# The second layer's weight conversion: its low part subtracted by VectorE in place of GpSimd

## The chip, the cores and the metric

The kernel runs on one core of a Trainium2 chip. Its time is that of the device in microseconds (us). The engines are named as in the profile: PE is TensorE (PEld its weight loads), DVE is VectorE, ACT is ScalarE, POOL is GpSimd, SP is SyncE, whose queue issues the DMAs.

## The reference

A linear attention with a decay per channel, then two layers of a gated MLP over 3072 tokens, all in float32:

```python
batch, n_heads, seq, head_dim = (4, 8, 768, 48)
n_tokens, d_model, d_ff = (3072, 384, 2048)
for t in range(S):
    state = alpha[:, :, t, :, None] * state + np.einsum('bhd,bhe->bhde', k[:, :, t], v[:, :, t])
    y[:, :, t] = np.einsum('bhd,bhde->bhe', q[:, :, t], state)
# first layer, x: (3072, 384), w_in: (384, 2048), w_out: (2048, 384)
h = x @ w_in
g = h * (1.0 / (1.0 + np.exp(-1.702 * h)))
x = g @ w_out
# second layer, with weights of its own
h = x @ w_in
g = h - np.tanh(h)
out = g @ w_out
```

## The kernel before

**Steps.** Each layer takes its 3072 tokens in 6 blocks of 512, and `d_ff` in 16 parts of 128. One block and one part are a step; `s` counts them, 96 for the first layer (s = 0 to 95) and 96 for the second (96 to 191). A step multiplies the block by 128 columns of `w_in` (`gemm1`, L343), puts the result through the layer's nonlinearity and multiplies that by 128 rows of `w_out` (`gemm2`, L350), three steps later (`LAG = 3`). Three accumulators (banks) take the sums of `gemm2` over the 16 parts.

**Two parts of every number.** For precision each operand is kept as a high and a low part, and a product is three matmuls: high by high, low by high, high by low. So a step is 9 matmuls of `gemm1` and 9 of `gemm2`, all 128 x 128 by 128 x 512. The high part is a rounding copy by ACT, the low part the difference. For the weights these are `whi[m]` and `wlo[m]`, 16 tiles of 128 x 768 each (the part's columns of `w_in` and its rows of `w_out` side by side). There is one set of them: the second layer's part m takes the tile of the first layer's part m, once the last block's `gemm2` with it is done.

**Conversion of a weight tile.** The weights arrive as 64-bit floats (`raw`, three buffers), and `conv` makes float32 of them with three passes of DVE (`w_bits`, L160 and L161, and `w_join`, L173) into one of four buffers `cf` (the fourth is in `arena`). Then `w_split` takes them apart: ACT copies the high part (L190), and the low part is a subtraction (L191), which the change touches. The first layer's 16 tiles are converted while attention runs, the second's 16 tiles in the last block of the first layer and the first steps of the second, about one in a step.

**What else DVE does in a step.** In a first-layer step it finishes the activation (`sig_1`: ACT's tanh, L357, then DVE's L358, which reads the bank of `gemm1`). The bank is one of two, so `gemm1` of step s + 2 waits for L358 of step s. Then `g_split` makes `ghi` (ACT, L361) and `glo` (L362; on DVE in the last block), which `gemm2` of step s needs. In a second-layer step L369 and L370 on ACT and L371 to L373 on DVE take the place of L357 and L358. GpSimd makes the low part of the second layer's input (`xlo`, L410).

**Order.** Instructions are written in the order of the steps, and a scheduler in the compiler that simulates time sets each engine's queue from it. Within a queue the order is fixed: an instruction that waits holds all behind it.

Of the kernel before, what the change touches and what calls it, by code (L numbers as in the profile page):

```python
# [7 lines left out]
F32 = mybir.dt.float32  # L8
# [5 lines left out]
ALU = mybir.AluOpType  # L14
# [54 lines left out]
def linear_attention_mlps(ctx, tc, xq, xv, fa, fv, cst, w1, w2, out):  # L69
    nc = tc.nc  # L70
    V, A, G, P, SP = nc.vector, nc.scalar, nc.gpsimd, nc.tensor, nc.sync
# [5 lines left out]
    def T(name, shape, dt=F32):  # L77
        return sb.tile(list(shape), dt, name=name)

    whi = [T(f"whi{m}", (128, WC), F32R) for m in range(MT)]  # L80
    wlo = [T(f"wlo{m}", (128, WC), F32R) for m in range(MT)]
# [106 lines left out]
    def w_split(l, m):  # L188
        f = cfs[l][m % len(cfs[l])]
        A.copy(whi[m], f)  # L190
        (V if l == 1 else G).tensor_tensor(out=wlo[m], in0=f, in1=whi[m].bitcast(F32), op=ALU.subtract)  # L191

# [221 lines left out]
    def conv(layer, split=True):  # L416
        if split and cv[2] < cv[1]:
            w_split(layer, cv[2] % MT)
            cv[2] += 1
        if cv[1] < cv[0]:  # L420
            m = cv[1] % MT
            w_join(layer, m)
            cv[1] += 1
            if m + 3 < MT:
                w_load(layer, m + 3)
        if cv[0] < min(layer * MT, cv[2] + len(cfs[layer])):
            w_bits(layer, cv[0] % MT)
            cv[0] += 1
# [51 lines left out]
    def place(s):  # L480
        l, j, m = steps[s]
        i = j if l == 1 else len(L1) + j
        t0, n = (L1 if l == 1 else L2)[j]
        alt = i >= len(L1) - 1 and (i - len(L1)) % 2
        return l, j, m, i, t0, n, [bank[b] for b in ((5, 6, 7) if alt else (0, 1, 2))]

    for s in range(NS + LAG):
        if s:
            if s <= NS:
                l, j, m, i, t0, n, acc = place(s - 1)  # L490
                prev = s - 1, n, V if l == 2 or j in (0, len(L1) - 1) else G
        if s < NS:
            l, j, m, i, t0, n, acc = place(s)
# [44 lines left out]
        if s >= LAG:  # L538
            l, j, m, i, t0, n, acc = place(s - LAG)
# [108 lines left out]
```

## Time and profile before

| | |
|---|---|
| median of 3 runs | 989.65 us (988.11 to 989.95) |
| profiled execution, its own time | 989.62 us |
| span of its instructions | 987.6 us |
| PE busy | 946.0 us (96%) |
| DVE, ACT, POOL busy | 616.1, 459.6, 229.7 us |
| mean granted clock of PE | 0.995 of full speed |

The span runs from the first to the last instruction; the execution is 2.0 us longer. Busy shares are means over the span. Matmuls overlap: one takes about 0.40 us in the records, but the next starts 0.23 us after it, so PE's pace is read from the distance of starts, and gaps from its waits.

### The profile page before, as it was taken

What the parts mean: (1) busy time and instruction counts of PE and PEld (TensorE: products, weight loads), DVE (VectorE), ACT (ScalarE), POOL (GpSimd) and SP (SyncE); (2) the same over time, 40 slices, a digit from 0 to 9 for tenths busy, and PEclk for the clock granted to TensorE, in tenths of its full rate; (3) what the DMA queues carried; (4) which work ended last, traced back from release to release, by engine and by line L of the source; (5) the groups of instructions that cost most, each with busy time, mean ns of one, the idle gap of its engine ahead of it and who ended that gap; (6) DMA issues with size and microseconds to landing.
All of it is one profiled execution on the core that took longest, in us unless ns stands there. A gap on an engine that the chain in (4) does not pass through costs nothing.

```text
span 987.6 us, 13249 instructions
## 1 busy us (share of the span) xinstructions
PE 946.0 (96%) x4870; PEld 739.4 (75%) x4870; DVE 616.1 (62%) x898; ACT 459.6 (47%) x969; POOL 229.7 (23%) x166
## 2 busy tenths in 40 slices
PE   6869999999999999999999889999999999999997
PEld 4656787777777777777787668888888888888885
DVE  7999743441443453643159987676777777766663
ACT  4445434333444534333343445554565656544542
POOL 1221302433544444343425450100100101000000
PEclk9999999999999999999999999999999999999999
DMA  9795212332455443752124330020132430000001
GB/s 285 239 313 158 72 53 58 99 89 84 131 183 182 152 139 105 268 164 73 49 78 150 124 128 1 6 91 0 59 133 90 140 100 25 33 1 1 33 0 37
DMA packets 58044, 101.85 MB, mean 103 GB/s; under 512 B 4992, under 2 KB 37376, under 8 KB 57968
## 3 DMA queue, kind: packets, MB, share of 16 engines
q1 hardware_dynamic: 57968, 100.90, 32.1%
q8 instruction: 40, 0.66, 0.3%
q14 instruction: 36, 0.29, 0.1%
HBM read 86.73 MB, written 14.16 MB: 102 GB/s over the span
## 4 chain that ended last, share of the span: by engine, by line
PE 82%; DVE 11%; DMA 3%; issue 3%; SPq 1%; ACT 0%; DVEq 0%; ACTq 0%
PE bank L350 38%; PE bank L343 38%; PE bank L273 3%; PE bank L305 2%; DMA arena<-xq 2%; DVE cf L160 2%; DVE cf L173 2%; DMA raw<-w 1%; DVE arena L237 1%; PE bank L302 1%; DVE cf L161 1%; DVE glo L362 1%; PE bank L312 1%; DVE gt L358 1%; DVE arena L173 1%
## 5 line engine op out<-in xcount | busy, mean ns | idle before, releaser
L343 PE MATMUL bank<-xhi,whi 128*128 128x512 f32 x576 | 231.5, 402 | 10.7 <-DVE gt L358 7.9
L361 ACT CAST ghi<-gt 128x512 fp32r<-128x512 f32 x192 | 119.0, 620 | 244.9 <-DVE gt L373 136.3
L343 PE MATMUL bank<-xlo,whi 128*128 128x512 f32 x576 | 230.6, 400 | 0.0
L350 PE MATMUL bank<-ghi,whi 128*128 128x512 f32 x576 | 229.4, 398 | 0.0
L343 PE MATMUL bank<-xhi,wlo 128*128 128x512 f32 x576 | 229.4, 398 | 0.0
L350 PE MATMUL bank<-ghi,wlo 128*128 128x512 f32 x576 | 228.4, 397 | 0.0
L350 PE MATMUL bank<-glo,whi 128*128 128x512 f32 x576 | 227.3, 397 | 0.0
L362 DVE TENSOR_TENSOR glo<-gt,ghi 128x512 fp32r<-128x512 f32 x128 | 97.3, 760 | 82.2 <-ACT ghi L361 77.0
L358 DVE SCALAR_TENSOR_TENSOR gt<-gt,bank 128x512 f32<-128x512 f32 x96 | 65.5, 682 | 127.3 <-ACT gt L357 123.8
L343 PEld LDWEIGHTS bank<-xhi,whi 128*128 128x128 f32 x576 | 109.3, 190 | 41.2 <-DVE gt L358 10.2
L343 PEld LDWEIGHTS bank<-xlo,whi 128*128 128x128 f32 x576 | 109.4, 190 | 27.0 <-issue 1.4
L343 PEld LDWEIGHTS bank<-xhi,wlo 128*128 128x128 f32 x576 | 109.3, 190 | 25.9 <-issue 0.6
L350 PEld LDWEIGHTS bank<-ghi,whi 128*128 128x128 f32 x576 | 108.3, 188 | 27.1 <-issue 1.2
L350 PEld LDWEIGHTS bank<-glo,whi 128*128 128x128 f32 x576 | 108.1, 188 | 25.9 <-DVE arena L243 0.2
L350 PEld LDWEIGHTS bank<-ghi,wlo 128*128 128x128 f32 x576 | 108.3, 188 | 25.5 <-issue 0.8
L362 POOL TENSOR_TENSOR glo<-gt,ghi 128x512 fp32r<-128x512 f32 x64 | 85.4, 1334 | 142.8 <-ACT ghi L361 119.0
L237 DVE TENSOR_TENSOR_SCAN arena<-arena,seg 112x516 f32<-112x516 f32 x46 | 62.3, 1354 | 37.2 <-DMA arena<-xq 36.3
L371 DVE SCALAR_TENSOR_TENSOR arena<-arena,bank 128x512 f32<-128x512 f32 x96 | 65.7, 684 | 29.0 <-ACT arena L369 27.8
L410 POOL TENSOR_TENSOR xlo<-arena,xhi 128x512 fp32r<-128x512 f32 x18 | 27.5, 1555 | 236.4 <-ACT xhi L409 187.5
L357 ACT ACTIVATE gt<-bank 128x512 f32<-128x512 f32 x96 | 57.0, 594 | 51.8 <-PE bank L343 51.1
L373 DVE SCALAR_TENSOR_TENSOR gt<-arena 128x512 f32<-128x512 f32 x96 | 69.7, 726 | 10.6 <-DVE arena L372 0.9
L369 ACT ACTIVATE arena<-bank 128x512 f32<-128x512 f32 x96 | 57.2, 596 | 34.0 <-PE bank L343 33.3
(86 smaller groups left out, 895.4 us busy)
## 6 DMA issues: line engine op xcount, KB each, us to landing
raw<-w SPq DMA_DIRECT2D x64, 768.0 KB, 4.6
arena<-xq SPq DMA_DIRECT2D x46, 224.0 KB, 3.0
arena<-xq SPq DMA_DIRECT2D x22, 451.5 KB, 5.6
xt<-arena SPq DMA_DIRECT2D x96, 48.0 KB, 2.9
xlo<-xt SPq DMA_DIRECT2D x24, 192.0 KB, 4.2
x1t<-xs SPq DMA_DIRECT2D x6, 768.0 KB, 5.2
arena<-x1t SPq DMA_DIRECT2D x6, 768.0 KB, 4.5
out<-xs SPq DMA_DIRECT2D x18, 256.0 KB, 2.3
```

Of the source, the lines that this page charges most:

```text
L173: V.scalar_tensor_tensor(out=f.bitcast(I32), in0=r[:, :, 0], scalar=29, in1=f.bitcast(I32), op0=ALU.logical_shift_right, op1=ALU.bitwise_or)
L237: V.tensor_tensor_scan(out=dec(g, n), data0=src(g, n), data1=seg, initial=0.0, op0=ALU.mult, op1=ALU.max)
L273: P.matmul(out=o[hh][:, i], lhsT=k[r, 2 * x + i], rhs=q[r, 2 * x + i], start=True, stop=True)
L343: P.matmul(out=h, lhsT=w[m][:, ws], rhs=x[:, k, :n], start=c == 0, stop=c == 3 * KT - 1)
L350: P.matmul(out=acc[k][:, :n], lhsT=w[m][:, ws], rhs=x[s % 3][:, :n], start=m == 0 and c == 0, stop=m == MT - 1 and c == 2)
L357: A.activation(out=th[i][:, :n], in_=h, func=AF.Tanh, scale=0.851)
L358: V.scalar_tensor_tensor(out=gf[i][:, :n], in0=th[i][:, :n], scalar=1.0, in1=h, op0=ALU.add, op1=ALU.mult)
L361: A.copy(ghi[s % 3][:, :n], gf[s % 2][:, :n])
L362: e.tensor_tensor(out=glo[s % 3][:, :n], in0=gf[s % 2][:, :n], in1=ghi[s % 3][:, :n].bitcast(F32), op=ALU.subtract)
L369: A.activation(out=u, in_=h, func=AF.Square, accum_out=usum[:, s - NS1 :][:, :1])
L371: V.scalar_tensor_tensor(out=p, in0=u, scalar=P3, in1=h, op0=ALU.mult, op1=ALU.mult)
L373: V.scalar_tensor_tensor(out=gf[i], in0=w, scalar=PD, in1=p, op0=ALU.add, op1=ALU.mult)
```

## The change

The low part of the second layer's weights is subtracted by DVE, as the first layer's was before:

```diff
     def w_split(l, m):
         f = cfs[l][m % len(cfs[l])]
         A.copy(whi[m], f)
-        (V if l == 1 else G).tensor_tensor(out=wlo[m], in0=f, in1=whi[m].bitcast(F32), op=ALU.subtract)
+        V.tensor_tensor(out=wlo[m], in0=f, in1=whi[m].bitcast(F32), op=ALU.subtract)
```

Sixteen instructions leave GpSimd's queue and join DVE's, and the scheduler places its other work anew around them, from the last block of the first layer to the first steps of the second. SP's queue is the same.

In the rows below `whi_63` to `whi_78` and `wlo_79` to `wlo_94` are the 16 tiles (m = 0 to 15), `cf_101` to `cf_103` and `arena` the four buffers, `raw_95` to `raw_97` the arriving weights, `bank_127` and `bank_128` the two banks of `gemm1`, `bank_129` to `bank_131` the accumulators, `ghi_109` to `ghi_111` and `glo_112` to `glo_114` the three buffers of the activation's parts.

DVE's queue in the last block of the first layer, where the first subtraction (m = 0) comes in ahead of the bits of tile m = 4 (- before, + after):

```order
 L362 TENSOR_TENSOR glo_114<-gt,ghi_111 128x512
+L191 TENSOR_TENSOR wlo_79<-cf_101,whi_63 128x768
 L160 TENSOR_SCALAR cf_101<-raw_96 128x768
-L358 SCALAR_TENSOR_TENSOR gt<-gt,bank_127 128x512
 L161 SCALAR_TENSOR_TENSOR cf_101<-raw_96,cf_101 128x768
-L362 TENSOR_TENSOR glo_112<-gt,ghi_109 128x512
+L358 SCALAR_TENSOR_TENSOR gt<-gt,bank_127 128x512
 L173 SCALAR_TENSOR_TENSOR cf_101<-raw_96,cf_101 128x768
-L358 SCALAR_TENSOR_TENSOR gt<-gt,bank_128 128x512
+L191 TENSOR_TENSOR wlo_80<-cf_102,whi_64 128x768
+L362 TENSOR_TENSOR glo_112<-gt,ghi_109 128x512
```

From here on each tile adds one L191 to DVE's queue, behind the work on a later tile.

DVE's queue at the end of the conversion, in the changed kernel, from `glo` of step 93 to `glo` of step 95; L358 here is that of step 95, L371 the second layer's first:

```order
L362 TENSOR_TENSOR glo_112<-gt,ghi_109 128x512
L160 TENSOR_SCALAR arena<-raw_95 128x768
L161 SCALAR_TENSOR_TENSOR cf_103<-raw_97,cf_103 128x768
L191 TENSOR_TENSOR wlo_91<-cf_101,whi_75 128x768
L362 TENSOR_TENSOR glo_113<-gt,ghi_110 128x512
L358 SCALAR_TENSOR_TENSOR gt<-gt,bank_128 128x512
L161 SCALAR_TENSOR_TENSOR arena<-raw_95,arena 128x768
L173 SCALAR_TENSOR_TENSOR cf_103<-raw_97,cf_103 128x768
L371 SCALAR_TENSOR_TENSOR arena<-arena,bank_127 128x512
L173 SCALAR_TENSOR_TENSOR arena<-raw_95,arena 128x768
L191 TENSOR_TENSOR wlo_92<-cf_102,whi_76 128x768
L362 TENSOR_TENSOR glo_114<-gt,ghi_111 128x512
```

Before, the same stretch of the queue had no L191, and both L173 stood ahead of their step's L362 and of L371.

PE's queue around `gemm2` of step 94 (part m = 14, `whi_77`), which now stands whole ahead of `gemm1` of step 97 (`whi_64`):

```order
 L350 MATMUL bank_129<-ghi_110,whi_77 128x512
 L350 MATMUL bank_129<-ghi_110,wlo_93 128x512
+L350 MATMUL bank_130<-ghi_110,whi_77 128x512
+L350 MATMUL bank_130<-ghi_110,wlo_93 128x512
+L350 MATMUL bank_131<-ghi_110,whi_77 128x512
+L350 MATMUL bank_131<-ghi_110,wlo_93 128x512
+L350 MATMUL bank_129<-glo_113,whi_77 128x512
+L350 MATMUL bank_130<-glo_113,whi_77 128x512
+L350 MATMUL bank_131<-glo_113,whi_77 128x512
 L343 MATMUL bank_128<-xhi_104,whi_64 128x512
```

Seven matmuls that stood behind `gemm1` of step 97 have moved ahead of it, so `glo` of step 94 (`glo_113`) is wanted earlier.

## Rows read from the trace of the kernel before

**Rows 1.** Page, busy us (share of the span), number of instructions.

```profile
PE 946.0 (96%) x4870; PEld 739.4 (75%) x4870; DVE 616.1 (62%) x898; ACT 459.6 (47%) x969; POOL 229.7 (23%) x166
```

**Rows 2.** Waits of PE from 505 to 600: total us, times, longest.

```profile
PE bank L343 <- DVE gt L358: 7.9, 5, 1.7
PE bank L343 <- DVE arena L371: 2.2, 1, 2.2
```

**Rows 3.** Windows: length, busy us of each engine, granted clock, DMA share, GB/s.

```profile
528.83:539.20 10.37, 9.19 (x39) 7.11 (x39) 10.30 (x12) 3.70 (x7) 4.77 (x3) 1.00 0.45 156
...
570.00:580.00 10.00, 6.74 (x23) 5.14 (x24) 9.14 (x9) 3.44 (x7) 6.51 (x3) 0.87 0.67 225
```

**Rows 4.** Timeline of PE: first matmul of gemm1 in steps 84, 88, 99.

```profile
508.22 0.39 PE L343 MATMUL bank<-xhi,whi 128*128 128x512 f32 x1
...
524.49 0.39 PE L343 MATMUL bank<-xhi,whi 128*128 128x512 f32 x1
...
583.19 0.40 PE L343 MATMUL bank<-xhi,whi 128*128 128x512 f32 x1
```

**Rows 5.** Chain of waits from 600 to 640: start, length, what.

```profile
604.12 2.10 PE bank L343 x9
```

**Rows 6.** Timeline of DVE from 526.2: start, length, instruction.

```profile
526.17 0.68 DVE L358 SCALAR_TENSOR_TENSOR gt<-gt,bank 128x512 f32<-128x512 f32 x1
526.77 0.55 DVE L160 TENSOR_SCALAR arena<-raw 128x768 int32<-128x768 int32 x1
527.36 0.96 DVE L161 SCALAR_TENSOR_TENSOR arena<-raw,arena 128x768 int32<-128x768 int32 x1
528.23 0.69 DVE L362 TENSOR_TENSOR glo<-gt,ghi 128x512 fp32r<-128x512 f32 x1
528.83 2.61 DVE L173 SCALAR_TENSOR_TENSOR arena<-raw,arena 128x768 int32<-128x768 int32 x1
531.36 2.19 DVE L160 TENSOR_SCALAR cf<-raw 128x768 int32<-128x768 int32 x1
533.48 0.67 DVE L358 SCALAR_TENSOR_TENSOR gt<-gt,bank 128x512 f32<-128x512 f32 x1
534.08 0.94 DVE L161 SCALAR_TENSOR_TENSOR cf<-raw,cf 128x768 int32<-128x768 int32 x1
535.05 0.96 DVE L173 SCALAR_TENSOR_TENSOR cf<-raw,cf 128x768 int32<-128x768 int32 x1
```

**Rows 7.** Timeline of POOL from 500 to 620.

```profile
508.46 1.85 POOL L191 TENSOR_TENSOR wlo<-cf,whi 128x768 fp32r<-128x768 f32 x1 [13.24 <-ACT whi L190]
...
528.38 4.76 POOL L191 TENSOR_TENSOR wlo<-cf,whi 128x768 fp32r<-128x768 f32 x2 [5.60 <-DVE arena L161]
...
566.51 4.99 POOL L410 TENSOR_TENSOR xlo<-arena,xhi 128x512 fp32r<-128x512 f32 x3 [2.32 <-issue]
```

**Rows 8.** Line L173 from 14 to 120: duration in ns min/median/max.

```profile
L173 DVE SCALAR_TENSOR_TENSOR xs<-raw,xs x6: 941/943/951, 41.0 to 94.0; 128x768 int32<-128x768 int32 x6
```

**Rows 9.** Line L191 on DVE (16 subtractions): what its engine waited for.

```profile
  ACT whi L190: 1.2, 1
```

**Rows 10.** Timeline of DVE in the first layer's conversion.

```profile
59.46 0.93 DVE L191 TENSOR_TENSOR wlo<-xs,whi 128x768 fp32r<-128x768 f32 x1
60.31 0.94 DVE L173 SCALAR_TENSOR_TENSOR cf<-raw,cf 128x768 int32<-128x768 int32 x1
```

**Rows 11.** Timeline of DVE from 566 to 572.

```profile
566.98 1.80 DVE L362 TENSOR_TENSOR glo<-gt,ghi 128x512 fp32r<-128x512 f32 x1
568.70 1.66 DVE L160 TENSOR_SCALAR arena<-raw 128x768 int32<-128x768 int32 x1
...
570.88 1.44 DVE L161 SCALAR_TENSOR_TENSOR arena<-raw,arena 128x768 int32<-128x768 int32 x1
```

**Rows 12.** Timeline of ACT: a wait for DVE ahead of a cast, and the cast.

```profile
526.94 0.62 ACT L361 CAST ghi<-gt 128x512 fp32r<-128x512 f32 x1 [2.00 <-DVE gt L358]
527.47 0.83 ACT L190 CAST whi<-cf 128x768 fp32r<-128x768 f32 x1
```

## The prediction

> **What bounds the kernel now.** I read the page first: PE is busy for 946.0 of 987.6 us [rows 1], so only a stretch in which PE waits has time to give. The waits of PE name one such place behind the attention: from 505 to 600 PE waits 10.1 us in all, five times for L358 and once for L371, both on DVE [rows 2]. These are the instructions that free the bank for `gemm1` two steps on.
>
> The window of one stretch, 528.83 to 539.20, shows who is at fault: DVE is busy for 10.30 of 10.37 us, PE for 9.19, ACT for 3.70 [rows 3]. So between about 518 and 577, while the second layer's weights are converted in the last block of the first layer, DVE sets the pace and PE follows.
>
> How much is lost there I take from PE's starts. A half step of 9 matmuls takes 2.10 us where PE never waits [rows 5], a step 4.20, a matmul 0.233. From the first matmul of step 88 at 524.49 to that of step 99 at 583.19 are 58.70 us [rows 4]; the queue of before has 196 matmuls between them, and 196 x 0.2333 = 45.7. Lost: **13.0 us**. The waits are 10.1 of it; the rest is the filling of PE's pipeline after each gap and a stretch at a lower clock, whose mean from 570 to 580 is 0.87 of full speed, between the level of 2.4 GHz and that of 1.2, just after PE's longest waits [rows 3]. Without the waits all 13.0 go; more can't be had from this stretch. In step 84, at 508.22, PE still ran at its own pace [rows 4].
>
> The timeline of DVE tells why it is slow. In two steps it does ten instructions. L173 and L160 start 2.53 and 2.12 us before the next one (528.83 to 531.36 to 533.48), while an undisturbed L160 takes 0.59 (526.77 to 527.36) and L161, which has L173's shape, 0.87 [rows 6]. POOL started two subtractions at 528.38 that last 4.76 us together [rows 7], just over these two instructions. In the first layer's conversion, where POOL does no such subtraction, L173 is steady at 0.943 us, not 2.61 [rows 6, 8]. So a subtraction on POOL holds up DVE: by 2.53 - 0.87 = 1.66 us and 2.12 - 0.59 = 1.53, together 3.19 in two steps.
>
> **The change part by part.** *Removed:* sixteen subtractions on POOL, and with them the hold-ups: about 1.6 us of DVE's time for each tile. *Added:* sixteen L191 on DVE. In the first layer the same instruction took 0.85 us from its start to the next (59.46 to 60.31) [rows 10]. So two steps of DVE go from 10.37 us to 10.37 - 3.19 + 2 x 0.85 = 8.88, one step from 5.18 to **4.44 us**. PE wants 4.20. DVE stays a little slower than PE, by 0.24 us a step, and the question is whether it falls far enough behind in the twelve steps to make PE wait.
>
> *Whether it does.* The first L191 can start at 508.46, where POOL's did, released by ACT's cast [rows 7]. From it to L358 of step 95 DVE's new queue has 68 instructions: 13 L191 at 0.85, 12 L160 at 0.59, 11 L161 and 10 L173 at 0.87, 11 L358 and 11 L362 at 0.60 (526.17 to 526.77, and 528.23 to 528.83) [rows 6, 10]: 11.1 + 7.1 + 9.6 + 8.7 + 6.6 + 6.6 = 49.6 us. So L358 of step 95 starts at 558.1 if nothing holds DVE up.
>
> Something still does: POOL's three L410 stay, at the end of the first layer. Before, they held up L362 by 1.80 - 0.69 = 1.11 us, L160 by 1.66 - 0.55 = 1.11 and L161 by 1.44 - 0.96 = 0.48 [rows 6, 11], 2.7 us in all. Counted in full, L358 of step 95 starts at 560.8 and is done at 561.5; `glo` of step 94, the instruction ahead of it, at 560.9. PE, at its own pace from 508.22, reaches the matmuls with this `glo` 235 matmuls later, at 563.05, and `gemm1` of step 97 after 238, at 563.75. Margins: 2.1 and 2.2 us. Two more follow. L371 of step 96 comes 0.60 + 0.87 + 0.87 behind that L358, starts at 563.2 and is done 0.7 later; it is due after 253 matmuls at 567.25. L362 of step 95 starts at 565.5 and is done at 566.2; it is due after 262 at 569.35. So PE waits nowhere, if the counts hold.
>
> *What can eat the margin.* Where a pass follows the one that it depends on directly, 0.97 us lie between the starts in place of 0.87 (534.08 to 535.05) [rows 6]; in twelve steps up to 1.2 us. The margin is then 0.9, and the hold-up by L410 is known from one occurrence. Bounds of what PE still loses: 0 (all due times met) and 2.7 (the hold-up by L410 shows in full, the margin gone). I take 0.8, nearer the lower one, as the counted margin is positive.
>
> *Moved at no cost:* ACT's casts stand earlier or later by a row or two; ACT is busy for 3.70 of 10.37 us [rows 3]. The waits that join DVE's queue are those for ACT's cast (rival 2). The weight loads follow each L173, which gets no later. In the second layer's first steps four L191 remain, 3.4 us of DVE; DVE has 2.5 us of L362 and L371 to L373 at some 0.6 each in a step of 4.20, so they fit in three steps.
>
> The sum against the profiled execution: 989.62 - 13.0 + 0.8 = **977.4 us**. The median of the runs, 989.65, is the same within 0.03.
>
> A rule that speaks against this: the Trainium skill, "Perfetto Trace Analysis", section "Optimizing Scalar/DVE Operations", says that where the vector engine is saturated, giving work to ScalarE or GpSimd may pay; the change does the reverse with a DVE busy for 99%. The same paragraph warns that the two share a port and that moving work between them might not help. In this trace the warning holds: the offload costs DVE 1.6 us a tile where doing the work costs 0.85. What the first half would give is rival 3.
>
> **The rivals.** *1. DVE still paces PE.* The margin is gone from the start, since DVE begins step 88 as late as before. Then PE loses 12 x 0.24 = 2.9 us and L410's 2.7: 989.62 - 13.0 + 5.6 = 982.2. For it: DVE at 4.44 us is slower than PE's 4.20. Against: in before PE did not wait until after 524.49 although DVE's steps took 5.18, so there was slack of some us.
>
> *2. A wait at the head of DVE's queue.* L191 waits for ACT's cast, which stands in ACT's queue behind L361, which waits for DVE's L358: a round trip that the POOL's queue absorbed. A step then takes 4.44 + w; it is as slow as before at w = 0.74, and slower from there. With the cast (0.83) and L361 (0.62) both waited for [rows 12], w = 1.45 and 12 x 0.71 = 8.5 us are lost: 998.1. For it: ACT did wait 2.00 us for L358 ahead of such a cast [rows 12]. Against: in the first layer, 16 such subtractions on DVE waited once, for 1.2 us [rows 9], and in the new queue L191 of a tile stands 7 to 18 rows behind its L173 for the tiles 4 to 12.
>
> *3. The hold-up isn't POOL's doing.* The long L173 and L160 would come from something else in this stretch, such as the weight loads (DMA share 0.45 [rows 3]), and stay; DVE then gets 12 x 0.85 = 10.2 us more: 999.8. Against: the first layer's conversion has such loads too, and a steady L173 [rows 8].
>
> **How the numbers follow.** PE keeps its pace or nearly: 0.75, 976 to 980. Rival 1: 0.17. Rival 2: 0.05. Rival 3: 0.03. The runs of before spread from 988.11 to 989.95, about 0.2% or 2 us, which is what a measurement can tell from no change. The lower end of the range is the full gain, 976.6, less 0.9 for that spread: 975.7. The upper end, 981.5, takes in rival 1 in large part; beyond it lie its worst cases and rivals 2 and 3. Faster by over 0.2% are the forecast and rival 1: 0.92. Rival 2 with a wait near 0.74 gives no difference: 0.02. Slower: 0.06, from rivals 2 and 3.
>
> **What would show it.** In the profile of the changed kernel from 510 to 570: L173 and L160 steady at about 0.95 and 0.55 us, except beside the three L410; sixteen L191 on DVE at about 0.94; DVE's steps 4.4 to 4.5 us apart; no wait of PE for L358, or one or two under 2 us near the change of layers; the granted clock at 1.00 there. Step 99 of `gemm1` should start near 570 in place of 583. The forecast is wrong if waits for ACT's cast stand ahead of L191 on DVE, if L160 or L173 stay over 2 us, or if PE waits at each second step as now.

## The result, and the profile after

The changed kernel takes 975.0 us (median of 4 runs, 974.41 to 976.49), the kernel before in the same comparison 988.88 (4 runs, 986.02 to 989.95); the ratio is 0.9871, interval 0.9849 to 0.9893. The forecast was 977.4, in a range of 975.7 to 981.5. The median lies 0.7 us under that range; but the kernel before was faster in these rounds too, 988.88 and not 989.65, and the ratio 0.9871 lies inside the range as a ratio, 0.9859 to 0.9918. The profiled execution took 975.30 us, its span is 973.2.

The busy line of the page, which answers to [rows 1]:

```profile
PE 940.9 (97%) x4870; PEld 739.7 (76%) x4870; DVE 606.0 (62%) x914; ACT 460.6 (47%) x969; POOL 191.7 (20%) x150
```

DVE has 16 instructions more and is busy for 10 us less; POOL has 16 fewer and is busy for 38 us less.

PE's waits from 490 to 600, where [rows 2] had 10.1 us, are gone: that answer has no row. Windows of the stretch (length, busy us of PE, PEld, DVE, ACT, POOL, granted clock, DMA share, GB/s), answering to [rows 3]:

```profile
528.00:538.00 10.00, 10.00 (x45) 8.10 (x44) 9.71 (x15) 4.63 (x7) 0.00 (x0) 1.00 0.47 159
...
558.00:568.00 10.00, 10.00 (x45) 8.11 (x44) 10.00 (x11) 5.89 (x11) 4.48 (x3) 1.00 0.40 114
568.00:578.00 10.00, 10.00 (x45) 8.11 (x44) 10.00 (x17) 7.05 (x15) 0.00 (x0) 1.00 0.51 202
```

DVE is still busy nearly all the time, but PE now is too, and its granted clock stays at 1.00, the upper of its two levels (2.4 GHz). The timeline of PE has the first matmul of `gemm1` of steps 84, 97, 98 and 99, as [rows 4] had it for some:

```profile
508.44 0.40 PE L343 MATMUL bank<-xhi,whi 128*128 128x512 f32 x1
...
563.75 0.40 PE L343 MATMUL bank<-xhi,whi 128*128 128x512 f32 x1
...
567.24 0.40 PE L343 MATMUL bank<-xhi,whi 128*128 128x512 f32 x1
...
570.02 0.40 PE L343 MATMUL bank<-xhi,whi 128*128 128x512 f32 x1
```

None waited. From step 84 to step 99 PE takes 61.58 us; before it was 583.19 - 508.22 = 74.97 [rows 4]. These 13.4 us (with one matmul fewer in between, 13.2 like for like) are nearly all of the 14.4 us by which the span is shorter.

DVE's timeline at the place shown in [rows 6], and where the three L410 of POOL come ([rows 11] before):

```profile
526.18 0.68 DVE L362 TENSOR_TENSOR glo<-gt,ghi 128x512 fp32r<-128x512 f32 x1
526.79 0.95 DVE L173 SCALAR_TENSOR_TENSOR arena<-raw,arena 128x768 int32<-128x768 int32 x1
527.65 0.55 DVE L160 TENSOR_SCALAR cf<-raw 128x768 int32<-128x768 int32 x1
528.12 0.68 DVE L358 SCALAR_TENSOR_TENSOR gt<-gt,bank 128x512 f32<-128x512 f32 x1
528.72 0.95 DVE L161 SCALAR_TENSOR_TENSOR cf<-raw,cf 128x768 int32<-128x768 int32 x1
529.59 0.95 DVE L191 TENSOR_TENSOR wlo<-cf,whi 128x768 fp32r<-128x768 f32 x1
...
557.54 2.06 DVE L191 TENSOR_TENSOR wlo<-cf,whi 128x768 fp32r<-128x768 f32 x1
559.52 1.79 DVE L362 TENSOR_TENSOR glo<-gt,ghi 128x512 fp32r<-128x512 f32 x1
561.24 0.68 DVE L358 SCALAR_TENSOR_TENSOR gt<-gt,bank 128x512 f32<-128x512 f32 x1
561.84 1.46 DVE L161 SCALAR_TENSOR_TENSOR arena<-raw,arena 128x768 int32<-128x768 int32 x1
...
564.09 0.68 DVE L371 SCALAR_TENSOR_TENSOR arena<-arena,bank 128x512 f32<-128x512 f32 x1
...
566.42 0.68 DVE L362 TENSOR_TENSOR glo<-gt,ghi 128x512 fp32r<-128x512 f32 x1
```

L173 and L160 are back at 0.95 and 0.55 us. The L358 at 561.24 is that of step 95, the L362 ahead of it is `glo` of step 94. POOL's timeline shows what is left beside them, where [rows 7] had subtractions:

```profile
557.07 5.41 POOL L410 TENSOR_TENSOR xlo<-arena,xhi 128x512 fp32r<-128x512 f32 x3 [61.46 <-ACT xhi L409]
```

And the waits ahead of L191, now 32 instructions on DVE, where [rows 9] had 1.2 us once:

```profile
  ACT whi L190: 1.8, 3
```

### The profile page after: what moved, and what is told of

Its sections match the earlier page's. It is cut to its first block, busy times and chain, and to the rows that moved or that the text cites. A ratio compares the mean times of both kernels' runs of the same rounds, so it can differ in the third digit from the quotient of the medians.

```text
span 973.2 us, 13227 instructions
## 1 busy us (share of the span) xinstructions
PE 940.9 (97%) x4870; PEld 739.7 (76%) x4870; DVE 606.0 (62%) x914; ACT 460.6 (47%) x969; POOL 191.7 (20%) x150
## 4 chain that ended last, share of the span: by engine, by line
PE 87%; DMA 5%; DVE 5%; issue 1%; ACT 1%; SPq 0%; POOL 0%; DVEq 0%; ACTq 0%
PE bank L350 40%; PE bank L343 40%; DMA arena<-xq 4%; PE bank L273 3%; PE bank L305 2%; DMA raw<-w 2%; DVE arena L237 1%; PE bank L302 1%; PE bank L312 1%; DVE cf L161 1%; DVE cf L173 1%; DVE wlo L191 0%; DVE cf L160 0%; DVE xs L173 0%; ACT arena L248 0%
## 5 line engine op out<-in xcount | busy, mean ns | idle before, releaser
L350 PE MATMUL bank<-glo,whi 128*128 128x512 f32 x576 | 223.8, 396 | 0.0
L358 DVE SCALAR_TENSOR_TENSOR gt<-gt,bank 128x512 f32<-128x512 f32 x96 | 65.5, 682 | 125.8 <-ACT gt L357 122.7
L362 DVE TENSOR_TENSOR glo<-gt,ghi 128x512 fp32r<-128x512 f32 x128 | 93.2, 728 | 79.4 <-ACT ghi L361 76.0
L362 POOL TENSOR_TENSOR glo<-gt,ghi 128x512 fp32r<-128x512 f32 x64 | 85.8, 1341 | 139.0 <-ACT ghi L361 127.8
L410 POOL TENSOR_TENSOR xlo<-arena,xhi 128x512 fp32r<-128x512 f32 x18 | 27.9, 1574 | 307.6 <-ACT xhi L409 307.6
L371 DVE SCALAR_TENSOR_TENSOR arena<-arena,bank 128x512 f32<-128x512 f32 x96 | 65.7, 685 | 30.4 <-ACT arena L369 29.7
L373 DVE SCALAR_TENSOR_TENSOR gt<-arena 128x512 f32<-128x512 f32 x96 | 68.3, 711 | 9.4
```

Of the source, the lines that this page charges most:

```text
L350: P.matmul(out=acc[k][:, :n], lhsT=w[m][:, ws], rhs=x[s % 3][:, :n], start=m == 0 and c == 0, stop=m == MT - 1 and c == 2)
L358: V.scalar_tensor_tensor(out=gf[i][:, :n], in0=th[i][:, :n], scalar=1.0, in1=h, op0=ALU.add, op1=ALU.mult)
L362: e.tensor_tensor(out=glo[s % 3][:, :n], in0=gf[s % 2][:, :n], in1=ghi[s % 3][:, :n].bitcast(F32), op=ALU.subtract)
L371: V.scalar_tensor_tensor(out=p, in0=u, scalar=P3, in1=h, op0=ALU.mult, op1=ALU.mult)
L373: V.scalar_tensor_tensor(out=gf[i], in0=w, scalar=PD, in1=p, op0=ALU.add, op1=ALU.mult)
L410: G.tensor_tensor(out=xlo[i][:, k], in0=xr[:, k], in1=xhi[i][:, k].bitcast(F32), op=ALU.subtract)
```

## The experiments

Each is an edit of the changed kernel, of `w_split` unless another place is named. Times are medians of the runs named; the ratio is to the kernel before, run in the same rounds (its median there was 987.3 to 989.3 us). An edit moves the lines below it by one to four.

### GpSimd subtracts as well

```diff
         V.tensor_tensor(out=wlo[m], in0=f, in1=whi[m].bitcast(F32), op=ALU.subtract)
+        if l == 2:
+            G.tensor_tensor(out=wlo[m], in0=f, in1=whi[m].bitcast(F32), op=ALU.subtract)
```

> VectorE subtracts the low part as in the changed kernel, and GpSimd subtracts the second layer's 16 low parts once more into the same tiles; nobody but TensorE waits for that, and only for the last tiles. Theory (GpSimd's subtraction holds up VectorE's passes, by about 1.6 us a tile): VectorE goes from 4.44 to about 6.0 us a step, 12 steps cost 19 us more, less the margin of 2 us: about 990 to 1000 us, L173 or L160 over 2 us again beside the subtractions. Rival (the hold-up is not GpSimd's; the gain came from the new order of the queues): 975 us, as the changed kernel, L173 steady at 0.95 us.

Measured: 993.44 us (4 runs, 992.63 to 995.15), ratio 1.0069 (1.0052 to 1.0085): slower than the kernel before. DVE has the same instructions as in the changed kernel; only POOL's are added. Its timelines, DVE's first, then POOL's:

```profile
526.95 0.68 DVE L364 TENSOR_TENSOR glo<-gt,ghi 128x512 fp32r<-128x512 f32 x1
527.55 2.59 DVE L161 SCALAR_TENSOR_TENSOR arena<-raw,arena 128x768 int32<-128x768 int32 x1
530.07 0.67 DVE L360 SCALAR_TENSOR_TENSOR gt<-gt,bank 128x512 f32<-128x512 f32 x1
...
532.87 2.32 DVE L364 TENSOR_TENSOR glo<-gt,ghi 128x512 fp32r<-128x512 f32 x1
...
537.92 2.60 DVE L173 SCALAR_TENSOR_TENSOR cf<-raw,cf 128x768 int32<-128x768 int32 x1
```

```profile
527.10 2.23 POOL L193 TENSOR_TENSOR wlo<-cf,whi 128x768 fp32r<-128x768 f32 x1 [3.70 <-DVE wlo L191]
532.56 2.08 POOL L193 TENSOR_TENSOR wlo<-cf,whi 128x768 fp32r<-128x768 f32 x1 [3.23 <-DVE wlo L191]
537.60 2.10 POOL L193 TENSOR_TENSOR wlo<-cf,whi 128x768 fp32r<-128x768 f32 x1 [2.96 <-DVE wlo L191]
```

Whatever DVE begins next when POOL's subtraction has begun is the one that is long: L161, L362 (here L364) or L173. L161 takes 2.52 us from start to start in place of 0.87, a hold-up of 1.65 as in [rows 6]. DVE waits for POOL nowhere in this stretch, so it is delayed by the longer passes alone. PE waits again, from 490 to 620 most of all for `glo` (total, times, longest):

```profile
PE bank L352 <- DVE glo L364: 8.1, 5, 2.5
PE bank L345 <- DVE gt L360: 4.6, 3, 3.2
```

Once a tile over twelve steps the hold-ups would be 19.8 us (some of the later ones are shorter, 1.0 to 1.3 us); by the ratios the kernel lost (1.0069 - 0.9871) x 988.9 = 19.6 us against the changed one. That the two agree so closely is chance, as the margin takes up the first of it and a lower clock adds to it (last section). But the hold-up is POOL's doing, and it is neither the place nor the order of DVE's passes.

### No subtraction, and half of them

```diff
-        V.tensor_tensor(out=wlo[m], in0=f, in1=whi[m].bitcast(F32), op=ALU.subtract)
+        if l == 1:
+            V.tensor_tensor(out=wlo[m], in0=f, in1=whi[m].bitcast(F32), op=ALU.subtract)
```

> The second layer's low parts are not subtracted at all (the first layer's stay in the tiles), so neither engine has the work. Theory (in the changed kernel TensorE already keeps its own pace through the conversion): 975 us, within 1 us of the changed kernel, no wait of TensorE between 505 and 600. Rival (VectorE's 4.4 us a step still cost something): 2 to 5 us below the changed kernel, 970 to 973 us.

Measured: 976.07 us (4 runs, 973.78 to 977.14), ratio 0.9884 (0.9865 to 0.9903), no wait of PE there. Taking the work away altogether gains nothing over putting it on DVE: the changed kernel has all that was to be had in this stretch.

```diff
-        V.tensor_tensor(out=wlo[m], in0=f, in1=whi[m].bitcast(F32), op=ALU.subtract)
+        (V if l == 1 or m % 2 == 0 else G).tensor_tensor(out=wlo[m], in0=f, in1=whi[m].bitcast(F32), op=ALU.subtract)
```

> Even tiles are subtracted by VectorE, odd ones by GpSimd. Theory: the hold-ups come with the odd tiles alone, VectorE needs 4.44 - 0.43 + 0.8 = 4.8 us a step on average, against TensorE's 4.18; the loss lies between nothing and half of what the kernel before loses: 976 to 982 us. Rival (any GpSimd subtraction in this stretch costs the full price because the queues are coupled): 986 us or more.

Measured: 978.49 us (4 runs, 976.17 to 980.65), ratio 0.9917 (0.9892 to 0.9941). With eight subtractions on POOL, PE waits once, for 3.3 us:

```profile
PE bank L343 <- DVE gt L358: 3.3, 1, 3.3
```

The price is not in proportion: by the ratios 0.0046 of the 0.0129 are lost again, about a third and not half. The margin can be what absorbs the rest; no run shows that.

### More work on DVE, none on GpSimd

```diff
-        V.tensor_tensor(out=wlo[m], in0=f, in1=whi[m].bitcast(F32), op=ALU.subtract)
+        for _ in range(l):
+            V.tensor_tensor(out=wlo[m], in0=f, in1=whi[m].bitcast(F32), op=ALU.subtract)
```

> VectorE subtracts each of the second layer's low parts twice into the same tile; GpSimd has none. Theory (what counts is VectorE's time for a tile, whoever causes it): 4.44 + 0.85 = 5.3 us a step, as slow as the kernel before (5.18): 12 x 0.85 = 10 us more VectorE work less the margin of 2 us, 983 to 990 us, TensorE waiting for L358 again. Rival (the loss of before was special to GpSimd, an engine that finishes late and so keeps buffers): 975 us.

Measured: 984.24 us (10 runs, 981.54 to 989.46), ratio 0.9969 (0.9949 to 0.999). In the profiled execution (986.55 us) PE waits again, though no subtraction runs on POOL:

```profile
PE bank L351 <- ACT ghi L362: 4.2, 1, 4.2
PE bank L344 <- DVE gt L359: 2.6, 3, 2.1
PE bank L344 <- DVE arena L372: 0.4, 1, 0.4
```

So a slower DVE is enough, without POOL: 0.85 us more a tile by DVE's own work brings back (0.9969 - 0.9871) / 0.0129, three quarters of the loss. That it is not all of it, though a step of DVE is counted at 5.3 us here and at 5.18 before, isn't explained. The longest wait is for ACT's cast (L362, `ghi`) of step 96, which in turn waits for what DVE does ahead of it.

```diff
         V.tensor_tensor(out=wlo[m], in0=f, in1=whi[m].bitcast(F32), op=ALU.subtract)
+        if l == 2:
+            V.tensor_tensor(out=wlo[m][:, :384], in0=f[:, :384], in1=whi[m][:, :384].bitcast(F32), op=ALU.subtract)
```

> As the changed kernel, and VectorE subtracts the first 384 of the 768 columns of each of the second layer's low parts once more: about 0.45 us more a tile, 5.4 us over twelve steps. Theory with the margin counted in the prediction (2.1 us, less 1.2 us for dependent passes): TensorE waits for 3 to 4.5 us, 978 to 980 us. Rival (the slack is wider than counted, for instance 5 us or more): 975 to 976 us.

Measured: 981.37 us (4 runs, 977.49 to 983.43), ratio 0.9948 (0.9929 to 0.9967). PE's waits in the profiled execution, the fastest of the four, come to 4.0 us:

```profile
PE bank L352 <- ACT ghi L363: 3.0, 1, 3.0
PE bank L345 <- DVE arena L373: 1.0, 2, 0.8
```

So the wider slack of the rival falls. Counted by the margin, 5.4 us of work less 1.8 (below) would make 3.6 us of waits, but that this is near 4.0 is chance: the scheduler put part of DVE's work behind L358 of step 95, which still ended 2.2 us ahead of `gemm1` of step 97 (559.02 and 561.25). The wait of 3.0 us is for `ghi` of step 96, a due time that the prediction didn't count. The other three runs were 3 to 6 us longer, and by the ratios 7.6 us were lost against the changed kernel, more than the work added; this profile doesn't explain that.

### What POOL does while DVE works

```diff
-        V.tensor_tensor(out=wlo[m], in0=f, in1=whi[m].bitcast(F32), op=ALU.subtract)
+        if l == 1:
+            V.tensor_tensor(out=wlo[m], in0=f, in1=whi[m].bitcast(F32), op=ALU.subtract)
+        else:
+            G.memset(wlo[m].bitcast(F32), 0.0)
```

> The second layer's low parts are not computed: GpSimd fills each tile with zeros in place of subtracting, an instruction that writes the same tile but reads nothing. Theory in the form of a port held for the whole instruction whatever it does: L160 and L173 are both held up by about the length of the fill. Rival form (only an instruction that reads on GpSimd holds up L173 and L362, which have two inputs in SBUF; L160, one input at a higher rate, is held up by either): L173 steady at 0.95 us, L160 over its 0.55 us where a fill runs. Time in either form 975 to 985 us, since the fill should be shorter than the subtraction.

Measured: 978.31 us (one run). No wait of PE from 490 to 600; step 84 began at 511.80 in place of 508.44, so the longer time comes from ahead of the stretch. The fills took 0.74 us each and fell beside L173 and L358, not beside L160, so this tells only half. The second version fills four times:

```diff
+            for _ in range(4):
+                G.memset(wlo[m].bitcast(F32), 0.0)
```

> The second layer's low parts are not computed: GpSimd fills each tile with zeros four times, about 3 us a tile, so that fills run beside every pass of VectorE. If an instruction that only writes leaves passes with two inputs alone but holds up the one with one input at the higher rate: L173, L161, L362 steady at 0.95 and 0.69 us, L160 longer than 0.56 us by up to 0.74 us, or fills that are longer by L160's time. If write-only work never meets VectorE: all four steady. If the port is held whatever the instruction does: all of them longer. Time 976 to 980 us, as TensorE has some us of margin.

Measured: 971.78 us (one run, within the scatter of the changed kernel, 971.19 to 976.53 in these rounds), no wait of PE there. From DVE's timeline, then POOL's:

```profile
534.36 0.88 DVE L160 TENSOR_SCALAR arena<-raw 128x768 int32<-128x768 int32 x1 [0.65 <-ACT whi L190]
535.16 0.67 DVE L366 TENSOR_TENSOR glo<-gt,ghi 128x512 fp32r<-128x512 f32 x1
535.75 0.94 DVE L161 SCALAR_TENSOR_TENSOR arena<-raw,arena 128x768 int32<-128x768 int32 x1
...
537.22 0.94 DVE L173 SCALAR_TENSOR_TENSOR arena<-raw,arena 128x768 int32<-128x768 int32 x1
```

```profile
533.28 3.43 POOL L195 MEMSET wlo<- 128x768 f32 x4 [0.76 <-PE bank L354]
...
558.23 11.91 POOL L195 MEMSET wlo<- 128x768 f32 x16
```

During the four fills, 533.28 to 536.71, L362 (here L366) and L161 keep their 0.67 and 0.94 us; only L160 is longer, 0.88 in place of 0.55 (so at every second tile; at the others it takes 0.59). The four fills take 3.43 us, not 4 x 0.74 = 2.96: 0.47 us more, about L160's own time, as if a fill waits for L160 as well. The sixteen fills from 558.23 on, with no L160 beside them, take 0.74 us each. So an instruction on POOL that only writes leaves the passes with two inputs in SBUF alone, and meets only L160, the pass with one input that runs at a higher rate. What the fill lacks beside the subtraction is the reading; it is shorter too, so these rows suggest that the reading is what holds up the passes with two inputs, and don't show it by themselves. The Trainium skill, "SBUF — State Buffer", section "Who interferes with whom", states this rule, and that the later one waits for the whole of the other's instruction. The rows agree with both: with GpSimd subtracting as well, L161 ends at 530.14, 0.81 us after POOL's subtraction (529.33), and it takes 0.95 by itself.

### The last of GpSimd's work there

In `x1_split`:

```diff
-        G.tensor_tensor(out=xlo[i][:, k], in0=xr[:, k], in1=xhi[i][:, k].bitcast(F32), op=ALU.subtract)
+        V.tensor_tensor(out=xlo[i][:, k], in0=xr[:, k], in1=xhi[i][:, k].bitcast(F32), op=ALU.subtract)
```

> As the changed kernel, with the low part of the second layer's input (L410) on VectorE too, so that GpSimd has nothing in the second layer. Theory: VectorE's hold-ups of 1.1 us beside L410 go, and 0.6 us each are added; TensorE waited nowhere there, so 975 us, no difference beyond the scatter of 1 to 2 us. Rival (the three L410 still cost TensorE's pace something): 971 to 973 us.

Measured: 973.94 us (4 runs, 973.26 to 974.6), ratio 0.9863 (0.9847 to 0.988). Its interval overlaps that of the changed kernel, so both were run in the same rounds:

> The changed kernel once more, on the same chip and in the same rounds as the next one, to compare the two. 974 to 976.5 us; no wait of TensorE from 505 to 600, second-layer matmuls 0.2325 us apart, since no lower clock comes ahead of them.

> The changed kernel with L410 on VectorE too. Theory (TensorE waits nowhere in the second layer with either, so L410's place is worth nothing): within 1 us of the changed kernel in the same rounds. Rival (VectorE without hold-ups helps still): 1 us or more below it with intervals that do not overlap.

Measured: the changed kernel 973.85 us (5 runs, 971.19 to 976.53), ratio 0.9853 (0.9827 to 0.9879); with L410 on DVE 976.44 (6 runs, 971.52 to 977.59), ratio 0.9871 (0.9845 to 0.9898). The intervals overlap, and the order is the other way round than in the first pair. No difference can be told, as for a place where PE waits for 0.2 us at most.

### The kernel before once more

> The kernel before once more, for a second profile. TensorE's matmuls in the second layer started 0.2333 us apart in the profile of before and 0.2325 us in that of the changed kernel. If that pace belongs to the single execution, it may come out at either value here; if the waits ahead of it set it, it is 0.2333 again. Time 986 to 990 us in either case.

Measured: 985.83 us (one run), with the same waits of PE for L358 (7.9 us) and 3.0 us in two for L371, and a pace of 0.2324 us from one matmul's start to the next in the second layer. What that says is in the last section.

## Why the prediction was right

**The place and the size.** All the loss was in the stretch named, and all of it went. The 13.0 us counted there are 13.2 between the two profiles. About 1.4 of them are a stretch at a lower clock, which not every execution has (last section): in the second profile of the kernel before, step 84 to step 99 lost 73.57 - 266 x 0.2324 = 11.8 us.

**DVE's time for a tile.** L191 took 0.87 us from its start to the next (529.59 to 530.46), 0.85 was taken. L358 of step 95 was counted to start at 558.1, and at 560.8 with the hold-up by L410; it started at 561.24. The difference of 0.4 us is a sum of three: the first L191 started 0.2 us later (508.65, not 508.46), the passes took some 0.7 more than counted, mostly three waits for ACT (0.24, 0.33 and 0.18), and 0.5 less of the hold-up by L410 came ahead of it.

**The hold-up by L410.** Counted as 2.70 us. It fell on L191, L362 and L161: 2.06 - 0.95, 1.79 - 0.68 and 1.46 - 0.95, together 2.73. It hit another instruction than before, for the same time. But that L161 stands behind L358 of step 95, so only 2.2 us delayed the latter.

**The due times.** `gemm1` of step 97 was due at 563.75 and started at 563.75; step 98 at 567.25 and 567.24. L358 of step 95 was done at 561.92, so 1.8 us were left of the 2.2 counted; `glo` of step 94 had 1.7 of the 2.1. But these weren't the tightest. The prediction counted no due time for `ghi`, ACT's cast, which `gemm2` wants first. Of step 96, the second layer's first, it stands behind L371 to L373 on DVE, and the changed kernel had 0.9 us left there (570.59 + 0.62 = 571.21, and 572.12):

```profile
570.59 0.62 ACT L361 CAST ghi<-gt 128x512 fp32r<-128x512 f32 x1
572.12 0.40 PE L350 MATMUL bank<-ghi,whi 128*128 128x512 f32 x1
```

With the subtraction doubled and with half of it done twice, PE's longest wait is for this `ghi`. So that PE waits nowhere was foreseen, but that the due time left out was met too is luck.

**The rivals.** Rival 1 (DVE still paces PE) falls: PE waits nowhere, and taking the subtraction out gains nothing. Rival 2 (waits for ACT's cast) falls: 1.8 us in three waits ahead of L191 in the whole kernel, where [rows 9] had 1.2. Rival 3 (the hold-up isn't POOL's) falls by the run in which POOL subtracts as well.

**The terms that were off.** The 0.8 us left for PE's waits measured 0. And 1.2 to 1.4 us came from a place that the sum didn't have: after step 99 the changed kernel needs 973.2 - 570.02 = 403.18 us, the one before 987.6 - 583.19 = 404.41, where the change has next to nothing to do. The second profile of the kernel before needs 403.6 there, so most of it belongs to the one execution (last section). Both terms, less 0.2 us by which step 84 came later, take 977.4 to the 975.3 of the profile. The price of a matmul, 0.2333 us, was taken from that slower stretch too; at the 0.2324 us of the changed kernel the loss of before is 58.70 - 196 x 0.2324 = 13.1, close to what was measured.

## What to carry to other kernels

Before work is put on GpSimd to spare a busy VectorE, look whether VectorE's own instructions grow longer beside GpSimd's: here an offloaded subtraction cost VectorE 1.65 us, and doing it 0.87. A rise in VectorE's share of busy time is no loss if each of its results still comes before TensorE wants it, and this can be counted from the order of the queues: 68 instructions on one side, 238 matmuls on the other, gave the margin to within 0.4 us. Every result that TensorE wants has to be on the list, ScalarE's casts behind VectorE too: the tightest one here was not. Past the margin more work shows (some 10 us more on VectorE cost 9.7 by the ratios), and a lower clock can add to it.

## What the runs showed of the hardware

**A lower clock around a wait, sometimes.** PE waits 2.25 us for L371 in the profile of before, up to 577.71. From 578 to 580 its granted clock is 0.50, the lower of its two levels (1.2 GHz), which makes the mean of 0.87 from 570 to 580 [rows 3]; the first matmul takes 0.80 us. The second profile of the same kernel has the same wait and keeps full speed (the first row and the windows row are of before, the last of the second profile):

```profile
577.71 0.80 PE L343 MATMUL bank<-xhi,whi 128*128 128x512 f32 x1 [2.25 <-DVE arena L371]
578.00:580.00 2.00, 2.00 (x5) 1.53 (x6) 1.21 (x3) 0.79 (x2) 0.00 (x0) 0.50 1.01 415
576.08 0.50 PE L343 MATMUL bank<-xhi,whi 128*128 128x512 f32 x1 [2.26 <-DVE arena L371]
```

The stretch from step 84 to step 99 took 74.97 us in the one and 580.13 - 506.56 = 73.57 in the other, so this dip cost 1.4 us. Of the other kernels with such waits, some show it (0.76 from 580 to 590 with the doubled subtraction, around a wait of 4.2 us), some not (a wait of 2.95 us with the half one more). What decides wasn't found.

**Two paces of TensorE at a granted clock of 1.00.** In the second layer a half step of 9 matmuls takes 2.10 us in the profile of before [rows 5] and 2.09 in that of the changed kernel; over 93 steps this is more than 1 us. The counts of PE and PEld tell the two apart, here in 20 us of the kernel before (87 and 86) and then of the changed one (88 and 87):

```profile
600.00:620.00 20.00, 20.00 (x87) 16.12 (x86) 14.58 (x22) 11.19 (x24) 0.00 (x0) 1.00 0.01 2
```

```profile
600.00:620.00 20.00, 20.00 (x88) 16.21 (x87) 13.01 (x20) 10.17 (x20) 0.00 (x0) 1.00 0.00 0
```

The slower pace (0.2333 us) came in three profiles: that of before, GpSimd subtracting as well, and VectorE subtracting twice. In all three the clock had dipped ahead of it (means of 0.87, 0.83 and 0.76 over 10 us), and before the dip the pace was 0.2324, which the expectations round to 0.2325. The second profile of before, without a dip, kept 0.2324. But the kernel with half of the subtractions on GpSimd dipped too (0.91 from 560 to 580) and went on at 0.2324. So the dip may bring the pace, and doesn't always; that stays open.
